# Attention and feed-forward on one core: work moved off GpSimd, layer norm moved a phase ahead, normalising moved behind both exps, closing tiles reordered

## The chip, the core and the metric

The kernel runs on one core of a Trainium2 chip. The core has TensorE (PE, matmuls), VectorE (DVE), ScalarE (ACT), GpSimd (POOL) and SyncE (SP), which here only issues transfers, and 16 DMA engines. Each engine works through its own list of instructions in order, and engines wait for each other by semaphores. The metric is the time of one execution on the device in microseconds.

## The reference

The input is normalised, goes through an attention in which each position sees itself and seven earlier positions two apart, and through a feed-forward net; the two results are multiplied and added to the input.

```python
def reference(A_x, A_wqkv, A_wo, B_x, B_w1, B_b1, B_w2, B_b2):   # x [1, 2048, 448], all bf16
    def _A_ref(x, wqkv, wo):
        H = 16; Dh = D // H;  W, dil = 8, 2
        q, k, v = ...                                   # (x @ wqkv), heads of 28
        idx = pos[:, None] - (jnp.arange(W) * dil)[None, :];  mask = idx >= 0
        ...
        logits = jnp.einsum("bhsd,bhswd->bhsw", q, kg) * Dh ** -0.5
        attn = _softmax(jnp.where(mask[None, None, :, :], logits, -1e9), axis=-1)
        o = jnp.einsum("bhsw,bhswd->bhsd", attn, vg)
        return o.transpose(0, 2, 1, 3).reshape(B, S, D) @ wo
    def _B_ref(x, w1, b1, w2, b2):                      # F = 1792
        h = _gelu(jnp.einsum("bsd,df->bsf", x, w1) + b1)
        return jnp.einsum("bsf,fd->bsd", h, w2) + b2
    x = A_x
    xn = _layernorm(x, axis=-1)
    s = _A_ref(xn, A_wqkv, A_wo)
    g = _silu(_B_ref(xn, B_w1, B_b1, B_w2, B_b2))
    return x + s * g
```

## The kernel before

**Tiles.** The 2048 rows are put in order of even and odd rows, so that the seven earlier positions become neighbours. They are worked on as 16 tiles of 128 rows (`t`), as four chunks of 512 columns (`c`, NC = 4) for the matmuls that need the transposed input, and as 17 attention units of QB = 121 queries (`b`), each with its 128 keys. `xnT` holds the normalised input transposed, `qT` and `kT` queries and keys transposed, `vw` the values of a unit with a column of ones ahead of each head, by which the attention matmul gives the softmax denominator too.

**Steps.** `ln_stats`, `ln_rstd`, `ln_apply`: mean and variance on VectorE (L157, L158), the reciprocal root by Ln and Exp on ScalarE (L161, L162), the normalising on VectorE (L165, with a small copy L168). `ln_tr`, `ln_put`: four transposes on TensorE (L173) and a copy out of PSUM. `qk_weights`: eight copies that lay the q and k weights `wraw` out anew as `wqk` (L183, VectorE). `q_job`, `k_job`, `v_job`: four matmuls each (L189, L204) and a copy out (q on VectorE, k and v on ScalarE). `qk_unit`: 16 small matmuls S (L296), and twice an exp on ScalarE (L301) with a mask multiply on VectorE (L303). `av_unit`: 16 small matmuls psO (L312), a `stream_shuffle` that spreads the denominator (`den`, L316), and `norm`, which is handed back to be placed later: Ln and Exp of den on ScalarE (L319, L320) and the multiply into `oT` on VectorE (L321). `feed_forward_1`: per chunk 14 output tiles of 512 columns (L225, L234), gelu on ScalarE (L240). `ffn2_job`: 14 matmuls (L258) and the bias add `y` on VectorE (L260). `silu_job`: Tanh on ScalarE (L264) and a multiply-add `g` on VectorE (L265). `wo_job`: four matmuls (L272), `sg` (L278) and the sum with x, `o_t` (L281), both on VectorE, then the store (L282).

**Order.** Everything from L368 on stands in a block in which TensorE, VectorE, ScalarE and GpSimd run in the order in which the code is written. SyncE's queue and what stands ahead of the block are put in place by a scheduler. The program is: a start (tiles 0 to 3, v 0 to 3, weight copies, q and k of chunk 0, the first tiles of FFN1); three phases c = 0, 1, 2, each of `feed_forward_1(c)`, with the transposes of the next chunk in it, and of five attention units, four of which have an `ffn2_job` and a q, k or v job beside them, while the fifth has two v jobs and the first tiles of the next FFN1; then `feed_forward_1(3)` and a closing with units 15 and 16 and the last four tiles. Exp and Ln are in one table set of ScalarE, Gelu and Tanh in another, so that each phase loads tables twice (L335, L363). In `qk_unit` the `norm` of the unit before is placed between the two exps (L305).

**PSUM.** The pool psA has two buffers (S, odd tiles of FFN1). The pool psB has four banks that go round among transposes, v, q, k, FFN1, ffn2, wo and psO (tag "B"): whoever takes a bank waits for the reader of its last content.

**GpSimd** sets constants: `late_constants` (L125) has 34 memsets for `vw`, the masks `mk`, the memset of `wo`, and then issues wo's 16 loads on its own queue. In the closing it adds `o_t` of tiles 13 and 14 (L461, L463).

## Time and profile before

| | us |
|---|---|
| median of 3 runs | 190.26 (189.57 to 190.98) |
| the profiled execution | 189.0 |
| its span | 187.2 |
| PE busy (matmuls) | 167.3 (89%) |
| PEld busy (weight loads) | 75.8 (40%) |
| DVE busy | 121.2 (65%) |
| ACT busy | 124.5 (66%) |
| POOL busy | 17.3 (9%) |

Busy time is summed over the whole span, and matmuls are pipelined, so a busy TensorE is not TensorE at its peak. A row of the timeline gives the start of a group of like instructions, how long the group took, engine, line, operation and tiles; in brackets stand the idle time of the engine just before it and what released it. Starts count from the start of the span. A row of the chain gives start, length and the work that the end of the program waited for. Lines (L...) are those of the kernel above.

### The profile page before, as it was taken

The numbers are of one execution on the slowest core, as the hardware profiler recorded it, in microseconds if no ns is written. First come the engines' busy times: TensorE is split into PE (matmuls) and PEld (weight loads), VectorE is DVE, ScalarE is ACT, GpSimd is POOL, SyncE is SP. The second block draws the span as 40 slices with busy tenths as digits, with TensorE's granted clock in tenths as the row PEclk, the third lists the DMA queues.
The fourth block names the chain that finished last, engine by engine and source line by source line (L and its number), as shares of the span: only waits on it lengthen the run. The fifth ranks groups of instructions, "written<-read, shape, count | busy, mean of one in ns | idle before, by whom it ended". The sixth has DMA issues, their size and how long they took to land.

```text
span 187.2 us, 3332 instructions
## 1 busy us (share of the span) xinstructions
PE 167.3 (89%) x1324; PEld 75.8 (40%) x1324; DVE 121.2 (65%) x255; ACT 124.5 (66%) x195; POOL 17.3 (9%) x75
## 2 busy tenths in 40 slices
PE   7759989999998699999998689999998999999940
PEld 2314334444443244344543334444443344454510
DVE  3875754838677577838775656828677426887693
ACT  3833297196778798377778895096877799753610
POOL 2088760000000000000000000000000000000022
PEclk9999999999999999999999999999999999999995
DMA  5999940000000000000000001000000000310012
GB/s 155 214 314 327 368 121 4 2 2 4 0 4 0 0 0 4 0 0 0 4 0 4 2 0 49 0 28 0 4 0 0 4 2 0 123 53 25 0 49 74
DMA packets 10831, 9.04 MB, mean 48 GB/s; under 512 B 2656, under 2 KB 10816, under 8 KB 10816
## 3 DMA queue, kind: packets, MB, share of 16 engines
q1 hardware_dynamic: 10016, 8.21, 14.5%
q0 software_dynamic: 512, 0.40, 0.8%
q8 instruction: 10, 0.16, 0.4%
q10 hardware_dynamic: 288, 0.23, 0.4%
q14 instruction: 5, 0.04, 0.1%
HBM read 7.00 MB, written 1.84 MB: 47 GB/s over the span
## 4 chain that ended last, share of the span: by engine, by line
PE 37%; ACT 35%; DVE 18%; DMA 3%; issue 2%; SPq 1%; POOL 0%; DVEq 0%; ACTq 0%; POOLq 0%
ACT E L301 13%; PE ps_h L225 12%; PE ps_qk L189 10%; ACT hT L240 7%; ACT den L320 5%; ACT den L319 4%; DVE E L303 4%; DMA wraw<-in_A_wqkv_dram 3%; PE ps_h L234 3%; PE psO L312 3%; PE ps_y L258 3%; PE S L296 3%; DVE g L265 2%; DVE sg L278 2%; ACT L363 2%
## 5 line engine op out<-in xcount | busy, mean ns | idle before, releaser
L240 ACT ACTIVATE hT<-ps_h,b1f 128x512 bf16<-128x512 f32 x56 | 34.4, 700 | 16.7 <-PE ps_h L234 15.9
L258 PE MATMUL ps_y<-w,hT 128*128 128x448 bf16 x224 | 45.1, 353 | 0.0
L225 PE MATMUL ps_h<-xnT,w 128*128 128x512 bf16 x168 | 41.5, 380 | 2.1 <-DVE oT L321 1.9
L301 ACT ACTIVATE E<-S 128x976 bf16<-128x976 f32 x34 | 32.8, 978 | 9.9 <-PE S L296 9.8
L189 PE MATMUL ps_qk<-xnT,wqk 128*128 128x512 bf16 x128 | 30.0, 380 | 2.0 <-DVE wqk L183 2.0
L303 DVE TENSOR_TENSOR E<-E,mk_gen 128x976 bf16<-128x976 bf16 x30 | 20.1, 669 | 14.3 <-ACT E L301 14.0
L258 PEld LDWEIGHTS <-hT 128*128 128x128 bf16 x224 | 20.7, 98 | 19.2
L225 PEld LDWEIGHTS <-w 128*128 128x128 bf16 x168 | 15.0, 98 | 22.9 <-issue 5.0
L189 PEld LDWEIGHTS <-wqk 128*128 128x128 bf16 x128 | 12.2, 98 | 17.0 <-DVE wqk L183 2.7
L321 DVE TENSOR_TENSOR oT<-psO,den 128x484 bf16<-128x484 f32 (+1 forms) x17 | 11.2, 661 | 11.7 <-ACT den L320 11.7
L265 DVE SCALAR_TENSOR_TENSOR g<-th,y 128x448 bf16<-128x448 bf16 x16 | 10.2, 672 | 11.0 <-ACT th L264 11.0
L192 DVE CAST qT<-ps_qk 128x512 bf16<-128x512 f32 x16 | 11.0, 686 | 9.4 <-PE ps_qk L189 9.3
L281 POOL TENSOR_TENSOR o_t<-x,sg 128x448 bf16<-128x448 bf16 x2 | 2.1, 1028 | 154.5 <-DVE sg L278 154.5
L204 PE MATMUL ps_v<-wv,xnT 128*128 128x448 bf16 x68 | 15.2, 353 | 0.1
L319 ACT ACTIVATE den<-den 128x484 f32<-128x484 f32 (+1 forms) x17 | 10.2, 601 | 6.8 <-DVE den L316 6.7
L272 PE MATMUL ps_s<-wo,oT 128*128 128x448 bf16 x64 | 13.8, 353 | 0.9 <-ACT hT L240 0.8
L316 DVE STREAM_SHUFFLE den<-psO 128x484 f32<-128x484 f32 (+1 forms) x17 | 11.8, 693 | 0.0
L192 ACT CAST kT<-ps_qk 128x512 bf16<-128x512 f32 x10 | 5.8, 582 | 8.5 <-PE ps_qk L189 4.9
L209 ACT CAST vw<-ps_v 128x448 bf16<-128x448 f32 x17 | 8.7, 534 | 3.9 <-PE ps_v L204 3.8
L264 ACT ACTIVATE th<-y 128x448 bf16<-128x448 f32 x16 | 8.6, 598 | 3.8 <-DVE y L260 3.8
L157 DVE BATCH_NORM_STATS2 st<-x 128x6 f32<-128x448 bf16 x16 | 9.7, 608 | 2.1 <-DMA x<-in_A_x_dram 2.1
L320 ACT ACTIVATE den<-den 128x484 f32<-128x484 f32 (+1 forms) x17 | 10.3, 605 | 0.5
(58 smaller groups left out, 155.1 us busy)
## 6 DMA issues: line engine op xcount, KB each, us to landing
out_dram<-o_t SPq DMA_DIRECT2D x16, 112.0 KB, 1.7
w<-in_B_w_dram SPq DMA_DIRECT2D x1, 1568.0 KB, 10.4
w<-in_B_w_dram SPq DMA_DIRECT2D x2, 672.0 KB, 7.7
x<-in_A_x_dram SPq DMA_DIRECT2D x3, 448.0 KB, 7.9
wraw<-in_A_wqkv_dram SPq DMA_DIRECT2D x1, 672.0 KB, 6.1
w<-in_B_w_dram SPq DMA_DIRECT2D x4, 112.0 KB, 6.1
wo<-in_A_wo_dram POOLq DMA_DIRECT2D x16, 24.5 KB, 4.8
wv<-in_A_wqkv_dram SPq DMA_DIRECT2D x1, 336.0 KB, 4.7
```

The lines of the kernel that those rows point to most:

```text
L189: nc.tensor.matmul(ps[:, :], wqk[:, kt, 16 * which + 4 * g:16 * which + 4 * g + 4, :], xnT[:, kt, LEAD + c * CH:LEAD + (c + 1) * CH], star ...
L192: copy((qT, kT)[which][:, g, LEAD + c * CH:LEAD + (c + 1) * CH], ps[:, :])
L204: nc.tensor.matmul(ps[:, :], xnT[:, kt, o:o + P], wv[:, kt, :], start=(kt == 0), stop=(kt == KT - 1))
L225: nc.tensor.matmul(ps[i][:, :], w1[:, kt, m * P:(m + 1) * P], xnT[:, kt, LEAD + c * CH:LEAD + (c + 1) * CH], start=(first and kt == 0), st ...
L240: nc.scalar.activation(hT[:, m, :], ps[i][:, :], ACT.Gelu_apprx_tanh, bias=b1f[:, m:m + 1])
L258: nc.tensor.matmul(ps[:, :], hT[:, m, tt * P:(tt + 1) * P], w2[:, m, :], start=(m == 0), stop=(m == MT - 1))
L265: nc.vector.scalar_tensor_tensor(out=g_sb[t % NG][:], in0=th[:], scalar=1.0, in1=y_sb[:, t % 4, 0:D], op0=ALU.add, op1=ALU.mult)
L272: nc.tensor.matmul(ps[:, :], oT[:, g, t * P:(t + 1) * P], wo[:, g, :], start=(g == 0), stop=(g == 3))
L301: nc.scalar.activation(ev, Sp[p2][:, :, :, 0:QW], ACT.Exp, scale=SCALE)
L303: nc.vector.tensor_tensor(out=ev, in0=ev, in1=mkb, op=ALU.mult)
L319: nc.scalar.activation(den[:, :, 0:n], den[:, :, 0:n], ACT.Ln)
L320: nc.scalar.activation(den[:, :, 0:n], den[:, :, 0:n], ACT.Exp, scale=-1.0)
```

## The change

1. GpSimd: `vw` becomes one tile, and its 34 memsets become two that stand early. The memsets of `wv`, `wraw`, `wo`, `qT`, `kT` and `mk_gen` go to VectorE; wo's 16 loads go to SyncE's queue; the cast of `b1f` goes to the end of `late_constants`; both `o_t` adds of the closing go to VectorE.
2. Layer norm: the statistics of tiles 4 to 7 stand among the q and k jobs of the start, and their `ln_apply` behind the first FFN1 tiles, ahead of `feed_forward_1(0)`. In the phases `ln_apply` of the next chunk but one stands in the first four units.
3. Units: `norm` of the unit before stands behind both exps. In the fifth unit a v job is placed between the exps, and the second v job ahead of `norm`.
4. Closing: tile 12's silu is made with Exp, Ln and Exp between the units' `norm`; matmuls and put of wo and ffn2 are apart and in another order.

```diff
-    vw = [big.tile([P, H, 32], BF16, name=f"vw_{b}") for b in range(NB)]
+    vw = big.tile([P, NB, H, 32], BF16, name="vw")
...
-    nc.gpsimd.memset(wv[64:128, 3, :].bitcast(U32), 0)
-    nc.gpsimd.memset(wraw[:, :, 2 * D:2 * D + 8].bitcast(U32), 0)
-    nc.gpsimd.memset(wraw[64:128, 3, 0:2 * D].bitcast(U32), 0)
+
+    nc.gpsimd.memset(vw[:, :, :, 0:1], 1.0)
+    nc.gpsimd.memset(vw[:, :, :, DH + 1:32], 0.0)
+    nc.vector.memset(wv[64:128, 3, :].bitcast(U32), 0)
+    nc.vector.memset(wraw[:, :, 2 * D:2 * D + 8].bitcast(U32), 0)
+    nc.vector.memset(wraw[64:128, 3, 0:2 * D].bitcast(U32), 0)
+    nc.vector.memset(wo[:, :, :].bitcast(U32), 0)
+    for tl in (qT, kT):
+        nc.vector.memset(tl[:, :, 0:LEAD].bitcast(U32), 0)
+        nc.vector.memset(tl[:, :, LEAD + S:LQ].bitcast(U32), 0)
+    for g in range(4):
+        for h in range(4):
+            r = (4 * g + h) * DH
+            nc.sync.dma_start(wo[32 * h + 1:32 * h + 1 + DH, g, :], A_wo[r:r + DH, :])
 
     def late_constants():
-        nc.gpsimd.tensor_copy(b1f[:], b1t[:])
-        for tl in (qT, kT):
-            nc.gpsimd.memset(tl[:, :, 0:LEAD].bitcast(U32), 0)
-            nc.gpsimd.memset(tl[:, :, LEAD + S:LQ].bitcast(U32), 0)
-        for b in range(NB):
-
-            nc.gpsimd.memset(vw[b][:, :, 0:1], 1.0)
-            nc.gpsimd.memset(vw[b][:, :, DH + 1:32], 0.0)
-
-        nc.gpsimd.memset(mk_gen[:], 1.0)
+
+        nc.vector.memset(mk_gen[:], 1.0)
...
-        nc.gpsimd.memset(wo[:, :, :].bitcast(U32), 0)
-        for g in range(4):
-            for h in range(4):
-                r = (4 * g + h) * DH
-                nc.gpsimd.dma_start(wo[32 * h + 1:32 * h + 1 + DH, g, :], A_wo[r:r + DH, :])
+        nc.gpsimd.tensor_copy(b1f[:], b1t[:])
...
+    def silu_exp_job(t):
+
+        e = work.tile([P, D], F32, name="se", tag="se", bufs=1)
+        nc.scalar.activation(e[:], y_sb[:, t % 4, 0:D], ACT.Exp, scale=-1.0)
+        nc.scalar.activation(e[:], e[:], ACT.Ln, bias=1.0)
+        nc.scalar.activation(e[:], e[:], ACT.Exp, scale=-1.0)
+
+        def put():
+            nc.vector.scalar_tensor_tensor(out=g_sb[t % NG][:], in0=e[:], scalar=2.0, in1=y_sb[:, t % 4, 0:D],
+                                           op0=ALU.mult, op1=ALU.mult)
+        return put
...
             if p2 == 0:
-                norm()
+                between()
...
                     ln_put(nx + j, ln_tr(nx + j), nc.vector.tensor_copy)
-                    if j + 2 < 4:
-                        ln_apply(nx + j + 2)
...
         for g in range(4):
             q_job(0, g)
+            if g == 3:
+                ln_stats(7)
+                ln_rstd(4, 4)
+            else:
+                ln_stats(4 + g)
             k_job(0, g)
+        ps = ffn1_even(0, 0)
         for t in range(4, 8):
-            ln_stats(t)
-        ln_rstd(4, 4)
-        ps = ffn1_even(0, 0)
-        ln_apply(4)
-        ln_apply(5)
+            ln_apply(t)
...
                 b = next(units)
-                E = qk_unit(b, norm)
+                E = qk_unit(b)
+                norm()
                 ffn2_job(4 * c + i)
                 beside[i]()
+                if n + 1 < NC:
+                    ln_apply(4 * n + 4 + i)
                 norm = av_unit(b, E)
             b = next(units)
-            E = qk_unit(b, norm)
-            v_job(4 * n + 2 + (c == 2))
-            v_job(4 * n + 3 + (c == 2))
+            va, vb = 4 * n + 2 + (c == 2), 4 * n + 3 + (c == 2)
+            E = qk_unit(b, lambda: v_job(va))
+            v_job(vb)
+            norm()
             ps = ffn1_even(n, 0)
             norm = av_unit(b, E)
             norm()
-            if n + 1 < NC:
-                ln_apply(4 * n + 4)
-                ln_apply(4 * n + 5)
         feed_forward_1(3, ps, [3, 4, 5, 6, 7])
         wo_job(8)
         E = qk_unit(15)
         ffn2_job(12)
-        wo_job(9)
+        s9 = wo_mm(9)
         norm = av_unit(15, E)
-        E = qk_unit(16, norm)
+        wo_put(9, s9)
+        E = qk_unit(16)
+        norm()
+        g12 = silu_exp_job(12)
         ffn2_job(13)
-        wo_job(10)
+        g12()
+        s10 = wo_mm(10)
         norm = av_unit(16, E)
         norm()
+        wo_put(10, s10)
         nc.scalar.preload_act_table_set(SET_GELU)
-        silu_job(12)
+        s11 = wo_mm(11)
+        y14 = ffn2_job(14, False)
+        wo_put(11, s11)
+        s12 = wo_mm(12)
+        ffn2_put(14, y14)
+        wo_put(12, s12)
         silu_job(13)
-        ffn2_job(14)
-        wo_job(11)
         silu_job(14)
-        wo_job(12)
-        ffn2_job(15)
         s13 = wo_mm(13)
-        wo_put(13, s13, nc.gpsimd)
+        wo_put(13, s13)
+        y15 = ffn2_job(15, False)
+        s14 = wo_mm(14)
+        s15 = wo_mm(15)
+        ffn2_put(15, y15)
+        wo_put(14, s14)
         silu_job(15)
-        wo_job(14, nc.gpsimd)
-        wo_job(15)
+        wo_put(15, s15)
```

VectorE in the start, where tiles 1 to 3 are normalised (xnb_75 to xnb_77; x_70 is the first chunk of x) and the weights are laid out anew. Before:

```order
L165 TENSOR_SCALAR xnb_75<-x_70,mv,rstd 128x448
L168 COPY xnb_75<-xnb_75 128x64
L157 BN_STATS st<-x_70 128x6
L158 BN_AGGR mv<-st 128x2
L165 TENSOR_SCALAR xnb_76<-x_70,mv,rstd 128x448
L168 COPY xnb_76<-xnb_76 128x64
L165 TENSOR_SCALAR xnb_77<-x_70,mv,rstd 128x448
L168 COPY xnb_77<-xnb_77 128x64
L183 COPY wqk<-wraw 128x512 x8
L192 CAST qT<-ps_qk 128x512 x4
```

After:

```order
L164 TENSOR_SCALAR xnb_75<-x_70,mv,rstd 128x448
L167 COPY xnb_75<-xnb_75 128x64
L156 BN_STATS st<-x_70 128x6
L157 BN_AGGR mv<-st 128x2
L125 MEMSET wraw 128x4x4
L164 TENSOR_SCALAR xnb_76<-x_70,mv,rstd 128x448
L167 COPY xnb_76<-xnb_76 128x64
L164 TENSOR_SCALAR xnb_77<-x_70,mv,rstd 128x448
L167 COPY xnb_77<-xnb_77 128x64
L182 COPY wqk<-wraw 128x512 x8
```

The memset of wraw's last columns, which stood on GpSimd, now stands on VectorE ahead of the normalising of tile 2.

ScalarE in the first phase, from the v copy of the fourth unit to the load of the gelu tables. Before:

```order
L209 CAST vw_86<-ps_v 128x16x28
L301 ACTIVATE E<-S 128x8x122
L319 ACTIVATE den<-den 128x484
L320 ACTIVATE den<-den 128x484
L301 ACTIVATE E<-S 128x8x122
L209 CAST vw_87<-ps_v 128x16x28
L209 CAST vw_88<-ps_v 128x16x28
L319 ACTIVATE den<-den 128x484
L320 ACTIVATE den<-den 128x484
L335 ACT_TABLE_LOAD
```

After:

```order
L208 CAST vw<-ps_v 128x16x28
L317 ACTIVATE E<-S 128x8x122
L208 CAST vw<-ps_v 128x16x28
L317 ACTIVATE E<-S 128x8x122
L208 CAST vw<-ps_v 128x16x28
L335 ACTIVATE den<-den 128x484
L336 ACTIVATE den<-den 128x484
L335 ACTIVATE den<-den 128x484
L336 ACTIVATE den<-den 128x484
L351 ACT_TABLE_LOAD
```

The fifth unit's two exps now have a v copy between them, and the Ln and Exp of the fourth unit stand behind both v copies, right ahead of those of the fifth.

VectorE at the end of the program, the last twelve rows. Before (g_100 to g_103 and g_111 are silu results, x_72 and x_73 chunks of x):

```order
L260 TENSOR_TENSOR y<-ps_y,b2bc 128x448
L278 SCALAR_TENSOR_TENSOR sg<-ps_s,g_111 128x448
L281 TENSOR_TENSOR o_t<-x_72,sg 128x448
L265 SCALAR_TENSOR_TENSOR g_102<-th,y 128x448
L278 SCALAR_TENSOR_TENSOR sg<-ps_s,g_100 128x448
L281 TENSOR_TENSOR o_t<-x_73,sg 128x448
L260 TENSOR_TENSOR y<-ps_y,b2bc 128x448
L278 SCALAR_TENSOR_TENSOR sg<-ps_s,g_101 128x448
L265 SCALAR_TENSOR_TENSOR g_103<-th,y 128x448
L278 SCALAR_TENSOR_TENSOR sg<-ps_s,g_102 128x448
L278 SCALAR_TENSOR_TENSOR sg<-ps_s,g_103 128x448
L281 TENSOR_TENSOR o_t<-x_73,sg 128x448
```

After:

```order
L294 SCALAR_TENSOR_TENSOR sg<-ps_s,g_84 128x448
L297 TENSOR_TENSOR o_t<-x_73,sg 128x448
L269 SCALAR_TENSOR_TENSOR g_85<-th,y 128x448
L269 SCALAR_TENSOR_TENSOR g_86<-th,y 128x448
L294 SCALAR_TENSOR_TENSOR sg<-ps_s,g_85 128x448
L297 TENSOR_TENSOR o_t<-x_73,sg 128x448
L264 TENSOR_TENSOR y<-ps_y,b2bc 128x448
L294 SCALAR_TENSOR_TENSOR sg<-ps_s,g_86 128x448
L297 TENSOR_TENSOR o_t<-x_73,sg 128x448
L269 SCALAR_TENSOR_TENSOR g_87<-th,y 128x448
L294 SCALAR_TENSOR_TENSOR sg<-ps_s,g_87 128x448
L297 TENSOR_TENSOR o_t<-x_73,sg 128x448
```

All the sums `o_t` of tiles 12 to 15 are VectorE's now, and the matmuls' results of one tile are taken up (sg, then o_t) ahead of the y of a later one; of the silu multiplies three stand in the last twelve, since that of tile 12 is no longer near them and those of 13 and 14 have come later.

## Rows read from the trace of the kernel before

**Rows 1.** The page, part 4: shares of the chain that ended last, by engine

```profile
PE 37%; ACT 35%; DVE 18%; DMA 3%; issue 2%; SPq 1%; POOL 0%; DVEq 0%; ACTq 0%; POOLq 0%
```

**Rows 2.** Timeline of the start: start, length, engine, line, work, count, [idle before, releaser]

```profile
0.93 0.27 DVE L96 MEMSET wz<- 128x256 uint32 x1 [0.93 <-PEq L478]
...
3.35 0.63 DVE L157 BATCH_NORM_STATS2 st<-x 128x6 f32<-128x448 bf16 x1 [2.14 <-DMA x<-in_A_x_dram]
...
7.33 0.37 DVE L165 TENSOR_SCALAR xnb<-x,mv,rstd 128x448 bf16<-128x448 bf16 x1
...
8.84 0.70 DVE L183 COPY wqk<-wraw 128x512 bf16<-128x512 bf16 x3 [0.19 <-DMA wraw<-in_A_wqkv_dram]
...
9.94 0.11 POOL L122 MEMSET wraw<- 128x16 uint32 x1 [8.10 <-DMA wraw<-in_A_wqkv_dram]
...
10.61 3.92 DVE L183 COPY wqk<-wraw 128x512 bf16<-128x512 bf16 x5 [1.07 <-POOL wraw L123]
...
10.84 1.03 PE L189 MATMUL ps_qk<-xnT,wqk 128*128 128x512 bf16 x4
...
13.44 0.27 POOL L135 MEMSET mk_gen<- 128x122 bf16 x1
...
13.90 6.27 PE L189 MATMUL ps_qk<-xnT,wqk 128*128 128x512 bf16 x28 [2.04 <-DVE wqk L183]
...
24.04 0.96 PE L173 MATMUL pT<-ident,xnb 128*128 128x128 bf16 x8 [0.62 <-DVE xnb L165]
```

**Rows 3.** The page, part 5: all shuffles of the denominator (busy, mean ns)

```profile
L316 DVE STREAM_SHUFFLE den<-psO 128x484 f32<-128x484 f32 (+1 forms) x17 | 11.8, 693 | 0.0
```

**Rows 4.** The chain that ended last, in a middle unit: start, length, work

```profile
49.99 0.61 ACT den L320
50.59 0.88 ACT E L301
```

**Rows 5.** Timeline of TensorE, the same unit

```profile
48.05 0.39 PE L296 MATMUL S<-qT,kT 28*128 28x122 bf16 x16
...
51.88 0.73 PE L312 MATMUL psO<-E,vw 128*32 128x122 bf16 x16
52.55 0.40 PE L296 MATMUL S<-qT,kT 28*128 28x122 bf16 x16
```

**Rows 6.** Timeline of TensorE and ScalarE at the ends of phases

```profile
57.05 0.39 PE L296 MATMUL S<-qT,kT 28*128 28x122 bf16 x16
...
60.36 0.96 ACT L209 CAST vw<-ps_v 128x448 bf16<-128x448 f32 x2
...
63.86 1.28 ACT L335 ACT_TABLE_LOAD   x1
...
64.90 0.97 PE L173 MATMUL pT<-ident,xnb 128*128 128x128 bf16 x8 [1.37 <-DVE xnb L165]
65.71 0.59 PE L225 MATMUL ps_h<-xnT,w 128*128 128x512 bf16 x2
...
111.17 1.69 PE L272 MATMUL ps_s<-wo,oT 128*128 128x448 bf16 x8 [0.76 <-ACT hT L240]
```

**Rows 7.** Timeline of VectorE in the closing

```profile
173.56 0.62 DVE L321 TENSOR_TENSOR oT<-psO,den 128x448 bf16<-128x448 f32 x1 [1.26 <-ACT den L320]
...
178.02 0.62 DVE L265 SCALAR_TENSOR_TENSOR g<-th,y 128x448 bf16<-128x448 bf16 x1
178.56 0.62 DVE L278 SCALAR_TENSOR_TENSOR sg<-ps_s,g 128x448 bf16<-128x448 f32 x1
179.21 0.39 DVE L281 TENSOR_TENSOR o_t<-x,sg 128x448 bf16<-128x448 bf16 x1
179.52 0.61 DVE L260 TENSOR_TENSOR y<-ps_y,b2bc 128x448 f32<-128x448 f32 x1
...
183.36 0.79 DVE L281 TENSOR_TENSOR o_t<-x,sg 128x448 bf16<-128x448 bf16 x1
```

**Rows 8.** Windows: stretch, length, busy PE, PEld, DVE, ACT, POOL, PEclk, DMA share, GB/s

```profile
182.80:187.20 4.40, 0.00 (x0) 0.00 (x0) 1.31 (x2) 0.00 (x0) 1.03 (x1) 0.50 0.20 68
```

More of the change, by code (lines that the diff above doesn't have):

```diff
@@ L208, in v_put @@
     def v_put(b, ps):
-        nc.scalar.copy(vw[b][:, :, 1:DH + 1], ps[:, :].rearrange("p (h c) -> p h c", h=H))
+        nc.scalar.copy(vw[:, b, :, 1:DH + 1], ps[:, :].rearrange("p (h c) -> p h c", h=H))
     def v_job(b):
@@ L252, in ffn1_odd, with ffn2_job @@
         return ps
-    def ffn2_job(t):
+    def ffn2_job(t, put=True):
         tt = t % 4
@@ L259, in ffn2_job, with ffn2_put @@
                              start=(m == 0), stop=(m == MT - 1))
-        nc.vector.tensor_tensor(out=y_sb[:, tt, 0:D], in0=ps[:, :], in1=b2bc[:], op=ALU.add)
+        if put:
+            ffn2_put(t, ps)
+        return ps
+    def ffn2_put(t, ps):
+        nc.vector.tensor_tensor(out=y_sb[:, t % 4, 0:D], in0=ps[:, :], in1=b2bc[:], op=ALU.add)
     def silu_job(t):
@@ L274, in wo_mm, with wo_put @@
         return ps
-    def wo_put(t, ps, eng=None):
+    def wo_put(t, ps):
         sg = work.tile([P, D], BF16, name="sg", tag="sg", bufs=3)
@@ L280, in wo_put, with wo_job, qk_unit @@
         o_t = work.tile([P, D], BF16, name="o_t", tag="o_t", bufs=3)
-        (eng or nc.vector).tensor_tensor(out=o_t[:], in0=xt(t), in1=sg[:], op=ALU.add)
+        nc.vector.tensor_tensor(out=o_t[:], in0=xt(t), in1=sg[:], op=ALU.add)
         nc.sync.dma_start(dram_rows(out_par, t, 1)[:, 0, :], o_t[:])
-    def wo_job(t, eng=None):
-        wo_put(t, wo_mm(t), eng)
-    def qk_unit(b, norm=lambda: None):
+    def wo_job(t):
+        wo_put(t, wo_mm(t))
+    def qk_unit(b, between=lambda: None):
         E = work.tile([P, 4, 4, P], BF16, name="E", tag="E", bufs=2)
@@ L311, in av_unit @@
             for h in range(4):
-                nc.tensor.matmul(psO[32 * h:32 * h + 32, g, 0:QW], vw[b][:, 4 * g + h, :],
+                nc.tensor.matmul(psO[32 * h:32 * h + 32, g, 0:QW], vw[:, b, 4 * g + h, :],
                                  E[:, h, g, 0:QW], start=True, stop=True)
```

## The prediction

> **What bounds the kernel now.** I read the page's chain first, then the stretches that it names. Of the chain that ended last TensorE holds 37%, ScalarE 35% and VectorE 18% [rows 1]: no engine is the bound alone, the chain changes hands, so I sum by stage what is on it. The sum is made against the profiled execution, 189.0 us (span 187.2, the rest around it); the median, 190.26, is 0.7% above it, so the result is scaled by 1.0067 at the end.
>
> In the start the reader is to see TensorE empty for 2.04 us at 13.90, for the copies of the q and k weights on VectorE. Three copies took 0.70 us together, five took 3.92: one of them stood still for some 3.0 us, and it came free when the dense run of GpSimd's memsets ended at 13.44 + 0.27 [rows 2]. In a middle attention unit TensorE's list begins anew every 52.55 − 48.05 = 4.50 us, and of this the 16 psO matmuls took 0.73, against 0.40 and 0.39 for the 16 S matmuls [rows 5]: TensorE waits 0.33 inside, for the mask of the second exp. That exp stands behind the Ln and Exp of the unit before [rows 4]. At the end of a phase 65.71 − 57.05 = 8.66 us pass from the fifth unit's S to the next full tile of FFN1, among them a wait of 1.37 for VectorE's layer norm [rows 6]. At the end VectorE is the last engine, up to 183.36 + 0.79 = 184.15 [rows 7].
>
> **Start: 34 small memsets gone, but one memset now on VectorE.** The stuck copy has nothing dense to stand behind any more: 3.0 us come free. But the memset of wraw's last columns, which waits for both loads of wraw and began at 9.94 on GpSimd, where 8.10 us of waiting hurt nobody [rows 2], stands in the new order on VectorE between the statistics of tile 3 and the normalising of tile 2. Behind it are queued the normalising of tiles 2 and 3 and the eight weight copies; behind those TensorE's transposes, v 1 to 3 and all q and k. That normalising began at 7.33 before; now it begins at 9.94 + 0.11 = 10.05. From it to the first q matmul there were 10.84 − 7.33 = 3.51 us of this chain's own work, so q may begin at 13.56. The copies begin 8.84 − 7.33 = 1.51 after it, at 11.56, and are done 8 x 0.23 later at 13.4: just in time. The 32 matmuls of q and k, at 6.27 / 28 = 0.22 each, end at 20.6; before, the last 28 began at 13.90 and FFN1 followed at about 20.1. So 0.5 is lost. TensorE's wait of 0.62 at 24.04 for tiles 4 and 5 goes, since their normalising now stands ahead of FFN1. Net gain 0.1.
>
> The other memsets moved to VectorE are some 1,700 words; by the row with 256 words in 0.27 us an estimate of 1.8 us. They are hidden by the 2.14 us that VectorE waits for x at 3.35 [rows 2]; without this cover they cost at most 1.8. I take zero, and 1.8 goes to the range. The two large memsets of vw and the late cast of b1f are on GpSimd, idle for 8 us there; wo's loads go to SP behind the x loads, and wo is first needed about 90 us later. These I cost at nothing, at most 0.3.
>
> The rule that bears on this is in the Trainium skill, SBUF — State Buffer, "SBUF: two separate sides": of VectorE and GpSimd whichever begins first holds the shared port pair for the whole instruction, and the other blocks until it is done. Read strictly, one memset can hold a copy for one memset's time only, the stuck 3 us would have another cause, and would stay. The trace differs: the copy sat through some forty memsets, which overlap, and not through one. By the rule the sum would be 2.8 worse; it is rival F.
>
> **Units: normalising behind both exps.** The second exp no longer waits for Ln and Exp of the unit before, about 1.2 us on ScalarE [rows 4]. So the mask and psO no longer hold TensorE, and the 0.33 goes: the unit is then bound by TensorE's own list, 4.17. Next late is the normalising itself: oT of the unit before comes some 0.9 later, and its PSUM bank is wanted by the ffn2 of the next unit. I find a margin of about 0.3 us, the closest point of the change. VectorE's list in a unit (two masks, oT, den, y, and now one ln_apply of 0.4 to 0.6) is about 3.9, so it stays under 4.17. Gain 0.33 in units 2 to 4 of the first two phases and two of the third: 8 x 0.33 = 2.6. Ends: nothing, and 8 x 0.5 if the exps pull the masks still further ahead.
>
> **Phase ends.** ln_apply leaves the stretch behind the fifth unit; what is late next is oT of the fifth unit itself, whose bank the second transpose needs. From S on: first exp at 0.4, exp 0.88, v copy 0.48, exp 0.88, v copy 0.48 (two took 0.96 [rows 6]), which is 3.1; Ln and Exp of the fourth unit at 0.6 each [rows 4], 4.3; its oT 0.62 [rows 7], 4.95; den of the fifth unit 0.69 [rows 3], 5.65; its Ln and Exp, 6.85; its oT, 7.5; four transposes, half of 0.97, and the next tile stands at about 7.9, against 8.66. Gain 0.8 in the first phase. In the second 0.2 is lost again, since the wo matmuls that follow waited 0.76 for gelu anyway, and that wait is not shortened as much [rows 6]: 0.6. In the third the next work is gelu: the table load began 63.86 − 57.05 = 6.8 after S in the first phase [rows 6], and would begin at 6.85 now: nothing. Together 1.4; bounds 0 to 2.7.
>
> **Closing.** Unit 16's normalising comes at the same moment, its oT at 173.56. After it VectorE has, in the new order, oT 0.62, six sg at 0.65, six o_t (five at 0.31, the last 0.39), two y at 0.53 and three g at 0.54 (start to start, [rows 7]): 9.1 us, so 182.7 instead of 184.15, if nothing of it waits. Gain 1.4. The three passes of the new silu of tile 12 are 3 x 0.6 of ScalarE, between the two units' normalising; they are covered while unit 16's psO and den are still under way. Without that cover they cost up to 1.8.
>
> **Sum.** 0.1 + 2.6 + 1.4 + 1.4 = 5.5; 189.0 − 5.5 = 183.5; scaled, 184.7 us.
>
> **Rivals.**
> A. The start is freed in full: the memset does not hold VectorE, or the loads of wraw end earlier now that nothing else is queued. Then q begins at 10.84 and another 2.7 is gained: 182.0. Against it: the load released GpSimd at 9.94, and nothing ahead of it in its queue is changed.
> B. TensorE's clock falls in the new empty stretch of the start, some 2.7 us before tile 2's transposes. At half rate 16 of the 32 matmuls would take 0.22 more each, 3.5: 188.2. For it: after the last matmuls the granted clock was 0.50, that is 1.2 GHz instead of 2.4 [rows 8]. Against it: after the empty 2.04 at 13.90 the 28 matmuls ran at 0.22 each [rows 2]. That idleness lowers the clock is also in the Trainium skill, TensorE: Matmul & The Clock Gate, "What's actually happening"; the trace agrees for the end of the span, and not for this shorter stretch.
> C. The units do not shorten, as the bank of the unit before last comes free too late and ffn2 waits where psO waited: 2.6 less, 187.3. For it: the margin of 0.3 is of the size of two instruction gaps. Against it: ScalarE and VectorE keep 0.3 to 0.6 of slack in a unit.
> D. The closing gains nothing, because the three passes delay unit 16's Ln, or TensorE's wo 12 to 15 arrive late: 186.1.
> E. The other side: the clock falls to half at each of the long waits that the change makes, the one of the start and one of about 1.7 for oT at the end of each of the first two phases. At 3.5 each, 10.5 against a gain of 5.5: 195.2. The second fall takes the gain away, the third decides. Against it: waits of 2.04 and 1.37 cost no clock before [rows 2, 6].
> F. The stuck copy stays: 2.8 more, 187.5.
>
> **How the numbers follow.** Forecast 0.55, A 0.05, B 0.10, C 0.10, D 0.09, E 0.05, F 0.06. The likeliest's own range is 183.2 to 186.3 (0.5 to 1.5 either way from the memsets, the phase ends and the closing). The range for 8 in 10 takes in A to D and F: 181.9 to 188.2; what it leaves out is E and the edges of A and B, about 0.15. One per cent, about what a measurement of this kernel can tell from no change, is 188.4 on the near side and 192.2 on the far side. Faster holds the forecast, A, C, D, F and half of B: 0.90; same the other half of B: 0.05; slower E: 0.05.
>
> **What would show it.** In the profile after: in the start VectorE's memset of wraw waiting for the DMA until about 9.9, eight copies in under 2.2 us, and the first q matmul near 13.5 with all q and k at 0.22; in a middle unit 16 psO matmuls in 0.4 and 4.2 us from S to S; at the first two phase ends about 7.9 from S to the next full tile and a wait for oT ahead of the second transposes; at the end VectorE without a gap from oT of unit 16 on. The prediction is wrong if the units still take 4.5, if a wait for oT stands ahead of ffn2, if q begins before 12 or after 15, or if any stretch with matmuls shows a granted clock near 0.5.

## The result and the profile after

The changed kernel takes 184.31 us (median of 4 runs, 183.85 to 185.27); the kernel before took 190.53 beside it (189.57 to 190.98). The ratio is 0.9687, 95% interval 0.9631 to 0.9742. The prediction was 184.7. The profiled execution took 184.2 with a span of 182.6, against 189.0 and 187.2. Beside the experiments the kernel before took 188.5 to 189.8 where the mean granted clock of TensorE over the execution was 0.986 to 0.994, and 190.6 to 192.0 where it was 0.979 to 0.983; its profiled execution (189.0, clock 0.988) is like the former, which is probably why the profiled executions lie 4.8 apart and the medians 6.2.

The S matmuls of the 17 units are good marks: from one S to another a stage can be measured in any of the kernels. The table is made of their starts in the timeline of TensorE (us; each kernel's profiled execution).

| | before | after | gained | forecast |
|---|---|---|---|---|
| first q matmul | 10.84 | 15.21 | −4.37 | −2.72 |
| first matmul of FFN1 | 20.02 | 22.12 | −2.10 | −0.5 |
| S of unit 0 | 38.75 | 39.71 | −0.96 | +0.1 |
| units 0 to 4 | 18.30 | 17.29 | 1.01 | |
| units 5 to 9 | 18.30 | 17.30 | 1.00 | |
| units 10 to 14 | 18.29 | 17.64 | 0.65 | the three: 2.6 |
| unit 4 to 5 (phase end and FFN1) | 22.57 | 21.78 | 0.79 | 0.8 |
| unit 9 to 10 | 25.77 | 25.15 | 0.62 | 0.6 |
| units 14 to 16 | 23.91 | 24.00 | −0.09 | 0 |
| unit 16 to the end of the span | 21.31 | 19.73 | 1.58 | 1.4 |
| together | 187.2 | 182.6 | 4.6 | 5.5 |

All terms but one came out to within 0.2; the start came out a microsecond worse. What stood in [rows 2] is now, in the timeline of the start (rows of VectorE and TensorE; "..." marks rows left out):

```profile
6.84 0.92 PE L203 MATMUL ps_v<-wv,xnT 128*128 128x448 bf16 x4
...
9.47 0.07 DVE L125 MEMSET wraw<- 128x16 uint32 x1 [2.01 <-DMA wraw<-in_A_wqkv_dram]
9.47 0.40 DVE L164 TENSOR_SCALAR xnb<-x,mv,rstd 128x448 bf16<-128x448 bf16 x1
...
9.93 0.61 PE L172 MATMUL pT<-ident,xnb 128*128 128x128 bf16 x4 [2.17 <-DVE xnb L164]
...
10.33 1.70 PE L203 MATMUL ps_v<-wv,xnT 128*128 128x448 bf16 x4
...
10.51 1.70 DVE L182 COPY wqk<-wraw 128x512 bf16<-128x512 bf16 x8
...
12.25 3.13 PE L203 MATMUL ps_v<-wv,xnT 128*128 128x448 bf16 x8
...
15.21 7.07 PE L188 MATMUL ps_qk<-xnT,wqk 128*128 128x512 bf16 x31
...
22.12 1.46 PE L224 MATMUL ps_h<-xnT,w 128*128 128x512 bf16 x6
```

The memset waits for the load on VectorE, the normalising of tile 2 behind it, TensorE 2.17 behind that: as forecast. The eight copies run without a stop. But v 0 took 0.92 for four matmuls ahead of the empty stretch, and v 1 took 1.70 behind it. The windows (columns as in [rows 8]) tell why: the granted clock fell in the stretch, between 8.0 and 8.5, and was 0.50, that is 1.2 GHz, until q began.

```profile
5.00:10.00 5.00, 1.72 (x13) 0.88 (x14) 2.82 (x12) 2.88 (x9) 0.00 (x0) 0.84 0.89 198
10.00:15.00 5.00, 5.00 (x20) 2.57 (x21) 2.31 (x12) 2.14 (x4) 1.47 (x6) 0.50 1.03 327
15.00:20.00 5.00, 4.95 (x24) 2.21 (x24) 3.08 (x7) 1.71 (x3) 0.00 (x0) 0.98 1.09 326
```

In a middle unit psO no longer waits (0.40 where [rows 5] had 0.73), and S follows S after 4.17:

```profile
48.67 0.39 PE L312 MATMUL S<-qT,kT 28*128 28x122 bf16 x16
...
52.51 0.40 PE L328 MATMUL psO<-E,vw 128*32 128x122 bf16 x16
52.84 0.40 PE L312 MATMUL S<-qT,kT 28*128 28x122 bf16 x16
```

At the phase end 64.87 − 57.00 = 7.87 pass where [rows 6] had 8.66, with the forecast wait for oT in the middle:

```profile
57.00 0.39 PE L312 MATMUL S<-qT,kT 28*128 28x122 bf16 x16
...
62.52 0.39 PE L172 MATMUL pT<-ident,xnb 128*128 128x128 bf16 x4
64.63 0.40 PE L172 MATMUL pT<-ident,xnb 128*128 128x128 bf16 x4 [1.73 <-DVE oT L337]
64.87 1.46 PE L224 MATMUL ps_h<-xnT,w 128*128 128x512 bf16 x6
```

In the closing VectorE runs from oT of unit 16 to the last sum in 179.33 + 0.39 − 170.48 = 9.24, nearly without a gap (forecast 9.14; [rows 7] had 10.59):

```profile
170.48 0.62 DVE L337 TENSOR_TENSOR oT<-psO,den 128x448 bf16<-128x448 f32 x1 [1.26 <-ACT den L336]
...
179.33 0.39 DVE L297 TENSOR_TENSOR o_t<-x,sg 128x448 bf16<-128x448 bf16 x1
```

### The profile page after: what moved, and what is told of

It is laid out like the page before. It is cut to its first block, busy times and chain, and to the rows that moved or that the text cites. A ratio compares the mean times of both kernels' runs of the same rounds, so it can differ in the third digit from the quotient of the medians.

```text
span 182.6 us, 3260 instructions
## 1 busy us (share of the span) xinstructions
PE 165.5 (91%) x1308; PEld 76.6 (42%) x1324; DVE 118.0 (65%) x266; ACT 125.3 (69%) x197; POOL 4.6 (2%) x16
## 3 DMA queue, kind: packets, MB, share of 16 engines
q1 hardware_dynamic: 10688, 8.61, 15.8%
## 4 chain that ended last, share of the span: by engine, by line
PE 60%; ACT 24%; DVE 8%; DMA 3%; issue 2%; SPq 1%; DVEq 0%
PE ps_y L257 18%; PE ps_qk L188 12%; PE ps_h L224 11%; ACT E L317 6%; PE ps_v L203 5%; ACT hT L239 5%; PE ps_s L288 4%; DMA wraw<-in_A_wqkv_dram 3%; PE S L312 3%; ACT den L336 3%; PE ps_h L233 3%; ACT den L335 2%; PE psO L328 2%; DVE sg L294 2%; DVE g L269 2%
## 5 line engine op out<-in xcount | busy, mean ns | idle before, releaser
L224 PE MATMUL ps_h<-xnT,w 128*128 128x512 bf16 x160 | 40.4, 380 | 0.6 <-DVE sg L294 0.2
L317 ACT ACTIVATE E<-S 128x976 bf16<-128x976 f32 x34 | 32.0, 986 | 7.3 <-PE S L312 6.3
L188 PE MATMUL ps_qk<-xnT,wqk 128*128 128x512 bf16 x120 | 29.2, 379 | 0.4
L224 PEld LDWEIGHTS <-w 128*128 128x128 bf16 x168 | 15.2, 98 | 20.1 <-issue 4.8
L269 DVE SCALAR_TENSOR_TENSOR g<-th,y 128x448 bf16<-128x448 bf16 x15 | 8.7, 621 | 13.7 <-ACT th L268 13.7
L203 PE MATMUL ps_v<-wv,xnT 128*128 128x448 bf16 x68 | 17.2, 392 | 0.0
L172 PE MATMUL pT<-ident,xnb 128*128 128x128 bf16 x64 | 6.1, 232 | 6.9 <-DVE oT L337 3.4
L233 PE MATMUL ps_h<-xnT,w 64*128 64x512 bf16 x56 | 9.9, 383 | 0.5 <-ACT hT L239 0.2
L294 DVE SCALAR_TENSOR_TENSOR sg<-ps_s,g 128x448 bf16<-128x448 f32 x16 | 9.9, 616 | 0.2
```

The costliest lines, as they stand in the source:

```text
L188: nc.tensor.matmul(ps[:, :], wqk[:, kt, 16 * which + 4 * g:16 * which + 4 * g + 4, :], xnT[:, kt, LEAD + c * CH:LEAD + (c + 1) * CH], star ...
L203: nc.tensor.matmul(ps[:, :], xnT[:, kt, o:o + P], wv[:, kt, :], start=(kt == 0), stop=(kt == KT - 1))
L224: nc.tensor.matmul(ps[i][:, :], w1[:, kt, m * P:(m + 1) * P], xnT[:, kt, LEAD + c * CH:LEAD + (c + 1) * CH], start=(first and kt == 0), st ...
L233: nc.tensor.matmul(ps[i][:, :], w1[r, 3, m * P:(m + 1) * P], xnT[r, 3, LEAD + c * CH:LEAD + (c + 1) * CH], start=first, stop=not first)
L294: nc.vector.scalar_tensor_tensor(out=sg[:], in0=ps[:, :], scalar=0.5, in1=g_sb[t % NG][:], op0=ALU.mult, op1=ALU.mult)
L317: nc.scalar.activation(ev, Sp[p2][:, :, :, 0:QW], ACT.Exp, scale=SCALE)
```

## Experiments

The kernel before ran beside each experiment (medians 189.2 to 190.7), so the kernels are compared by their ratio to it, and stages by one profiled execution of each.

### The start: the clock, the memset, the small memsets

**a_busy.** Nine matmuls of zeros fill the empty stretch.

```diff
         v0 = v_mm(0)
+        busy(9)
```

> The changed kernel with nine more matmuls of zeros (512 columns) behind v 0, in the stretch in which TensorE stands empty from 7.76 to 9.93 in the start; their result is read by nobody. Theory: the clock fell in that stretch, and that cost 12 v matmuls 0.19 each and the transposes some 0.2. With the stretch filled they run at full rate, the first q matmul stands near 12.9 instead of 15.21, and the time is 184.3 - 2.2 = 182.1. Rival: the v matmuls were slow for another cause (the transfers at full load there, or the copies out of PSUM): they stay at 0.38, and the time stays 184.3.

Measured: 182.78, ratio 0.9642 (0.9588 to 0.9696). The intervals of this ratio and of the changed kernel's overlap; the timeline of the start shows the difference (VectorE's memset first, then TensorE):

```profile
10.07 0.07 DVE L125 MEMSET wraw<- 128x16 uint32 x1 [2.57 <-DMA wraw<-in_A_wqkv_dram]
...
7.63 2.11 PE L347 MATMUL ps_w<-wz 128*128 128x512 bf16 x9
...
10.80 0.92 PE L203 MATMUL ps_v<-wv,xnT 128*128 128x448 bf16 x4
...
11.78 1.98 PE L203 MATMUL ps_v<-wv,xnT 128*128 128x448 bf16 x8
13.60 7.07 PE L188 MATMUL ps_qk<-xnT,wqk 128*128 128x512 bf16 x32
20.51 1.46 PE L224 MATMUL ps_h<-xnT,w 128*128 128x512 bf16 x6
```

With the stretch filled, v 1 to 3 run at full rate, and from the release of the memset (10.07 here, 9.47 in the changed kernel) to the first q matmul there are 3.53 us and not 5.74. The forecast chain had 3.51. The clock cost 2.2 us; the load, which landed 0.6 later in this execution, took a part of it back.

**a_tail.** The one memset goes back to GpSimd, all else as changed.

```diff
-    nc.vector.memset(wraw[:, :, 2 * D:2 * D + 8].bitcast(U32), 0)
+    nc.gpsimd.memset(wraw[:, :, 2 * D:2 * D + 8].bitcast(U32), 0)
```

> The changed kernel with one line different: the memset of wraw's last columns is back on GpSimd. Theory: nothing holds VectorE, tile 2 is normalised at 7.4, there is no empty stretch and no fall of the clock; the copies begin when wraw has landed (about 9.5) and the first q matmul stands at 10.5 to 11, FFN1 at 17.6 to 18.1 instead of 22.12: 4.0 to 4.5 less, 179.8 to 180.3. Rival: the weights and the x of FFN1 and of tiles 4 to 7 are not there before about 20, so that FFN1 waits for transfers: 2.1 less, 182.2. Second rival: the wait only moves to the copies, TensorE is empty from about 9 to 11 and the clock falls all the same: 183 to 184.

Measured: 181.20, ratio 0.9547 (0.9481 to 0.9612). This is 1.4 points better than the changed kernel, but some 1 us short of the theory. The empty stretch is gone; q stands at 12.41 and not at 10.5 to 11:

```profile
6.91 1.70 PE L203 MATMUL ps_v<-wv,xnT 128*128 128x448 bf16 x4
...
10.61 1.97 PE L203 MATMUL ps_v<-wv,xnT 128*128 128x448 bf16 x8
12.41 7.23 PE L188 MATMUL ps_qk<-xnT,wqk 128*128 128x512 bf16 x32
...
16.28 0.63 DVE L156 BATCH_NORM_STATS2 st<-x 128x6 f32<-128x448 bf16 x1 [2.11 <-DMA x<-in_A_x_dram]
```

Here v 0 and v 1 ran at half rate from the outset. That belongs to the execution and not to the edit: a_best below has the same start and its first q matmul at 10.85. The statistics of tile 4 wait 2.11 for x on VectorE, with a q copy queued behind them; from the first q matmul to FFN1 7.06 us pass, against 6.91 in the changed kernel. So the rival of the loads holds for 0.15 us here (7.68 pass in a_best, where q begins earlier).

**b_gps and b_gps_tail.** The kernel before with part 1 of the change alone, but for the two sums of the closing, which stay on GpSimd; and the same with that one memset left on GpSimd (the line of a_tail).

> The kernel before with the GpSimd part of the change alone (34 memsets to two, memsets to VectorE, wo's loads to SyncE). Theory: the start loses as in the changed kernel: TensorE empty for 2.2 us before tile 2's transposes, clock at half until about 15, FFN1 at about 22 and not 20.0: 2 us more, 192.3 to 192.8 against 190.5. Rival: the stuck copy was worth more than the stall: 188 to 190.5.

> The same part alone, but with the memset of wraw's last columns left on GpSimd. Theory: the copies run without a stop, the first q matmul stands at 10.8 and the 28 behind it follow at once: 3.0 less at the start of q and k, of which TensorE's waits for x of tiles 4 to 7 may give back a part: 187.5 to 188.5 against 190.5. Rival: FFN1 then waits for its weights: 190.5.

Measured: b_gps 190.64, ratio 1.0066 (1.0022 to 1.0109), slower by less than a per cent; the 0.9 to 1.2 per cent that were expected lie at the edge of the interval. In its profiled execution, 1.2 above that median, S of unit 0 stands 2.9 later than before and the first q matmul at 15.80; v 0 took 1.70 there, half rate ahead of the empty stretch already. b_gps_tail took 186.65, ratio 0.9821 (0.9742 to 0.9900), an interval that holds what was expected; S of unit 0 stands 2.2 earlier. Its timeline:

```profile
6.83 0.92 PE L203 MATMUL ps_v<-wv,xnT 128*128 128x448 bf16 x4
...
10.88 7.07 PE L188 MATMUL ps_qk<-xnT,wqk 128*128 128x512 bf16 x31
17.78 1.46 PE L224 MATMUL ps_h<-xnT,w 128*128 128x512 bf16 x6
```

One line turns the GpSimd part from a small loss into a gain; the two medians lie 2.1% apart.

**b_two.** The 34 memsets become two in the place where they stood (`vw` is one tile).

```diff
-            nc.gpsimd.memset(vw[b][:, :, 0:1], 1.0)
-            nc.gpsimd.memset(vw[b][:, :, DH + 1:32], 0.0)
+        nc.gpsimd.memset(vw[:, :, :, 0:1], 1.0)
+        nc.gpsimd.memset(vw[:, :, :, DH + 1:32], 0.0)
```

> The kernel before with the 34 memsets of vw made two in the same place on GpSimd (272 and 816 elements, 1.3 us each in the changed kernel), all else as before. Theory: what held the weight copy was a dense run of GpSimd instructions that overlap: two memsets that follow each other hold it for up to 2.5 us, so little is gained, 0.5 to 1: 189.5 to 190.0. Rival (one instruction is waited for, then the copy goes): at most one memset of 1.3 holds it: 1.7 less, 188.8. Second rival: memsets do not hold it at all: the copies take as long as before, 190.5.

Measured: 189.14, ratio 0.9975 (0.9930 to 1.0020): nothing that shows. The copies on VectorE (the last line has the shortest, median and longest of the eight in ns) and the memsets beside them:

```profile
10.59 3.91 DVE L181 COPY wqk<-wraw 128x512 bf16<-128x512 bf16 x5 [0.81 <-POOL wraw L123]
...
11.31 1.28 POOL L130 MEMSET vw<- 128x272 bf16 x1
12.19 1.58 POOL L131 MEMSET vw<- 128x816 bf16 x1
13.65 0.22 POOL L133 MEMSET mk_gen<- 128x122 bf16 x1
...
L181 DVE COPY wqk<-wraw x8: 274/290/3016, 9.1 to 14.1; 128x512 bf16<-128x512 bf16 x8
```

The longest copy takes 3.02 as before (3.03), beside a series of GpSimd instructions of which each begins ahead of the end of the last, whether they are many or few. It ends at 14.02, 0.15 after the memset of `mk_gen`, the last of the series; in the kernel before it ends at 13.85, 0.14 after the same memset. In both the next GpSimd instruction begins only behind the end of this one. So it is not the number of memsets, nor is one instruction waited for, as the first rival had it. The second rival has the time right, but not the cause: in b_gps_tail, with the memsets gone from beside them, the same eight copies take 2.12 together. Which instructions of the series can hold a copy is not shown. Part 1 gains by having moved the memsets to a time when VectorE waits for x.

### Units and phase ends

**b_norm.** The normalising behind both exps alone, in the kernel before.

```diff
-                E = qk_unit(b, norm)
+                E = qk_unit(b)
+                norm()
                 ffn2_job(4 * c + i)
...
-            E = qk_unit(b, norm)
+            E = qk_unit(b)
             v_job(4 * n + 2 + (c == 2))
             v_job(4 * n + 3 + (c == 2))
+            norm()
```

> The kernel before with one part of the change alone: the normalising behind both exps in the four units and behind the two v copies in the fifth. Theory: 8 units at 4.17 and not 4.50, 2.7 less; the phase ends gain nothing or lose up to 0.5 each, since ln_apply still stands there and oT of the fourth unit comes later: 188.0 to 189.0 against 190.5. Rival: the bank of the unit before last comes free too late without layer norm's move and the units stay at 4.5: 190.5.

Measured: ratio 0.9929 (0.9879 to 0.9979), under one per cent. The units take 17.29, 17.30 and 17.64 from first to fifth, to 0.01 those of the changed kernel: this part alone makes the units' 2.66. But the stages of the phase ends grow from 22.57 to 24.24 and from 25.77 to 26.56, far more than the 0.5 that was expected. VectorE and TensorE at the first:

```profile
62.70 0.66 DVE L321 TENSOR_TENSOR oT<-psO,den 128x484 bf16<-128x484 f32 x1 [1.31 <-ACT den L320]
63.28 0.39 DVE L165 TENSOR_SCALAR xnb<-x,mv,rstd 128x448 bf16<-128x448 bf16 x1
...
63.73 0.96 PE L173 MATMUL pT<-ident,xnb 128*128 128x128 bf16 x8 [1.99 <-DVE xnb L165]
64.53 2.21 PE L225 MATMUL ps_h<-xnT,w 128*128 128x512 bf16 x6
66.67 1.03 PE L234 MATMUL ps_h<-xnT,w 64*128 64x512 bf16 x4
```

The later oT pushes ln_apply, which stands behind it, and the transposes wait for that; but from S of the fifth unit they come only 0.09 later than before (7.94 against 64.90 − 57.05 = 7.85). The other 1.58 lie behind them: after the empty 1.99 the granted clock was 0.50 from about 65.1 to 68.5, and the first six matmuls of FFN1 took 2.21 where the changed kernel has 1.46. At the second phase end it is the same: 0.08 ahead of the transposes, 0.71 behind, clock 0.50 from about 106.1 to 109.5 after an empty 1.99. So it is TensorE's clock that gives back most of what the units gained.

**a_between.** The changed kernel with the normalising between the exps again.

```diff
-                E = qk_unit(b)
-                norm()
+                E = qk_unit(b, norm)
```

> The changed kernel with the normalising of the unit before placed between the two exps again, in the four units of a phase alone (the fifth unit and the closing as changed). Theory: a unit takes 4.50 again and not 4.17, 16 psO matmuls 0.73 and not 0.40: 8 x 0.33 = 2.7 more, 187.0. Rival: the units became shorter because layer norm left the stretches around them: 184.3.

Measured: 188.19, ratio 0.9922 (0.9883 to 0.9962). The units take 18.86, 18.86 and 18.31, together 3.8 more than in the changed kernel, and not 2.7. The units of the third phase, which have no ln_apply, are as before; those of the other two are longer than before by 0.56 in all, because ln_apply now stands on VectorE ahead of the shuffle of den, for which the Ln between the exps waits on ScalarE. In the unit that begins at 44.55 this wait is 0.51, and psO waits for the mask:

```profile
49.34 0.39 PE L328 MATMUL psO<-E,vw 128*32 128x122 bf16 x14 [0.62 <-DVE E L319]
```

So alone, normalising behind both exps brought 2.7 in the units and lost 2.5 at the phase ends (b_norm); beside the layer norm's move it is worth 3.8 in the units and loses nothing there. The layer norm's move without it (a_between, which keeps the new order of the fifth unit) costs 1.1 in the units against the kernel before, and gains 1.4 at the phase ends.

**a_slow.** Each unit's normalising made some 0.6 us later.

```diff
             nc.scalar.activation(den[:, :, 0:n], den[:, :, 0:n], ACT.Exp, scale=-1.0)
+            nc.scalar.copy(den[:, :, 0:n], den[:, :, 0:n])
```

> The changed kernel with a copy of den onto itself on ScalarE (some 0.6 us) between each unit's Exp and its oT. It measures how much later oT can come before a unit grows. Theory: the margin is about 0.3, so a unit grows by 0.3 from 4.17 and the four units of a phase take 18.2 and not 17.3; the two phase ends grow by up to 1.2 each and the closing by 0.6. Rival: the margin is over 0.6, and the units stay at 17.3.

Measured (one profiled execution): units 17.51, 17.50 and 17.75, some 0.05 more each and not 0.3. So oT may come about 0.55 later before a unit grows; the margin of 0.3 was an underestimate. The two phase ends grow by 2.9 and 1.3, and both waits for oT there from 1.73 to 2.84 and 2.83:

```profile
66.53 0.60 PE L172 MATMUL pT<-ident,xnb 128*128 128x128 bf16 x4 [2.84 <-DVE oT L338]
66.93 2.76 PE L224 MATMUL ps_h<-xnT,w 128*128 128x512 bf16 x6
...
108.70 0.40 PE L172 MATMUL pT<-ident,xnb 128*128 128x128 bf16 x4 [2.83 <-DVE oT L338]
```

The two waits are alike, the outcome is not: behind the first the granted clock was 0.50 from about 66.6 to 70.0, behind the second it stayed at 1.00 and the same six matmuls of FFN1 took 1.46. The fall cost 1.6. The two stages behind unit 14 grow by 1.25 and 1.24, without a fall; for the closing 0.6 was expected.

### Closing, and two ways to a faster kernel

**a_close.** The changed kernel with the closing's former order (its calls as in lines 442 to 464 of the kernel before), but norm behind both exps and all sums on VectorE.

> The changed kernel with the order of the closing of before (tile 12's silu by Tanh, wo and ffn2 jobs in one piece each), but with normalising behind both exps and all sums on VectorE as in the changed one. Theory: the closing's gain, 1.58 by the two traces (from the S of unit 16 to the end 21.31 before, 19.73 after), goes, less what GpSimd's two slow sums had cost: 185.0 to 185.9. Rival: the gain came from taking the two sums of 1.03 each off GpSimd alone: 184.3.

Measured: 185.64, ratio 0.9788 (0.9731 to 0.9844). By stages of the profiled execution, the quickest of its four, 20.28 pass from unit 16 to the end, against 19.73 with the new order and 21.31 before. So of the 1.58 the order and the new silu make 0.55, and what a_close shares with the changed kernel 1.03: 0.22 up to oT of unit 16, the other 0.81 behind it, where the two sums no longer stand on GpSimd. In a_close VectorE still waits 1.26 for the table load and Tanh behind oT:

```profile
170.57 0.62 DVE L337 TENSOR_TENSOR oT<-psO,den 128x448 bf16<-128x448 f32 x1 [1.26 <-ACT den L336]
172.46 1.16 DVE L269 SCALAR_TENSOR_TENSOR g<-th,y 128x448 bf16<-128x448 bf16 x2 [1.26 <-ACT th L268]
```

In the kernel before, beside the two sums on GpSimd, one g on VectorE took 1.43 and not 0.62, and the last o_t 0.79 and not 0.39 [rows 7]:

```profile
180.75 1.03 POOL L281 TENSOR_TENSOR o_t<-x,sg 128x448 bf16<-128x448 bf16 x1 [153.38 <-DVE sg L278]
180.83 1.43 DVE L265 SCALAR_TENSOR_TENSOR g<-th,y 128x448 bf16<-128x448 bf16 x1 [0.17 <-ACT th L264]
...
182.87 1.03 POOL L281 TENSOR_TENSOR o_t<-x,sg 128x448 bf16<-128x448 bf16 x1 [1.09 <-DVE sg L278]
```

**a_best and a_best2.** a_tail with the second tile's transposes behind the next FFN1 tiles, to fill the wait of 1.73; and the same with two more matmuls of zeros in the start.

```diff
                 ps = ffn1_even(c, k)
                 gelu(k, ps)
+                if k == 2 and c + 1 < NC:
+                    ln_put(nx + 1, ln_tr(nx + 1), nc.vector.tensor_copy)
...
-                for j in (k, k + 1):
+                for j in ((0,), (2, 3))[k // 2]:
```

> The kernel of a_tail, and in each phase the transposes of the next chunk's second tile stand behind the next two tiles of FFN1 instead of ahead of them. Theory: the wait of 1.73 for oT of the fifth unit, which the change made at two phase ends, is filled with FFN1; from the S of the fifth unit to the next phase's first S 20.05 instead of 21.78 in the first phase, and 23.4 instead of 25.15 in the second; 3.4 less than a_tail: 177.8. Rival: the wait moves to gelu on ScalarE, which cannot begin before the table load behind the fifth unit's Exp, and FFN1 stops at its next tile for a free PSUM buffer: 0.5 to 1 less each, 179.5 to 180.

> The kernel of a_best with two more matmuls of zeros in the start: nine instead of eight ahead of the first transposes, and one behind them, where TensorE stood empty for 0.4 and 0.6. Theory: in a_tail the first eight v matmuls took 0.37 each and the rest 0.23, so the clock came up only near 10.6, and what keeps TensorE from standing empty before brings it up sooner: the first q matmul at 10.9 and not at 12.4, 1.5 less: 176.3. Rival: when the clock comes up is a matter of the execution and not of these gaps: as a_best.

Measured: 182.40, ratio 0.9582 (0.9485 to 0.9680), and 182.38, ratio 0.9586 (0.9506 to 0.9667). Both miss: they are no faster than a_tail. The stages of the phase ends grow to 23.12 and 25.49: the wait for oT is gone, 0.58 for gelu has come, and 1.73 for a copy of xnT that now stands on VectorE behind the g of two silu jobs:

```profile
62.56 0.37 PE L233 MATMUL ps_h<-xnT,w 64*128 64x512 bf16 x1 [0.58 <-ACT hT L239]
...
64.74 1.16 DVE L269 SCALAR_TENSOR_TENSOR g<-th,y 128x448 bf16<-128x448 bf16 x2 [3.20 <-ACT th L268]
65.82 1.32 DVE L176 COPY xnT<-pT 128x512 bf16<-128x512 bf16 x3
...
66.29 0.38 PE L172 MATMUL pT<-ident,xnb 128*128 128x128 bf16 x4 [1.73 <-DVE xnT L176]
```

In both the first q matmul stands at 10.85 or 10.81, where a_tail with the same start has 12.41, so what the two extra matmuls do can't be told from what differs between executions.

**a_all.** a_best2 with the silu jobs behind that copy, and the statistics of tiles 4 to 7 behind the third and fourth k job.

```diff
                 gelu(k, ps)
+                if k == 2:
+                    if c + 1 < NC:
+                        ln_put(nx + 1, ln_tr(nx + 1), nc.vector.tensor_copy)
+                    if c:
+                        silu_job(4 * (c - 1))
+                        silu_job(4 * (c - 1) + 1)
...
             k_job(0, g)
+            if g == 2:
+                ln_stats(4)
+            if g == 3:
+                for t in (5, 6, 7):
+                    ln_stats(t)
+                ln_rstd(4, 4)
```

> The kernel of a_best2 with two mends: the silu jobs that stood ahead of the second tile's copy out of PSUM on VectorE stand behind it, and the statistics of tiles 4 to 7, which waited for x with a q copy queued behind them, stand behind the third and fourth k job. Theory: of the waits that a_best showed, 0.62 for the q copy and 1.73 for the copy of xnT go and 0.58 for gelu stays: FFN1 at 17.8 to 18.0, 20.6 from the S of the fifth unit to the next phase's S (21.78 in the changed kernel, 23.12 in a_best) and 24.0 (25.15, 25.49); 181.2 - 1.5 - 2.3 = 177.4. Rival: Tanh, now behind two more gelus, makes ScalarE late at the next FFN1 tiles, and the phase ends gain nothing: 179.7.

Measured: 180.29, ratio 0.9533 (0.9437 to 0.9629), 2.9 above the theory. FFN1 begins at 17.82 as expected, the first phase end gains 0.55 against the changed kernel (21.23), and the second loses 0.67 (25.82): the wo matmuls there now wait 2.17 for gelu, where in the changed kernel they waited 0.95 for a copy of xnT.

```profile
104.88 1.68 PE L288 MATMUL ps_s<-wo,oT 128*128 128x448 bf16 x8 [2.17 <-ACT hT L239]
```

a_all and a_tail beat both kernels; by their intervals they can't be told apart, and a_tail is one line.

## Why the prediction was right, and where it was not

**Right: units, phase ends, closing.** The units' 0.33 is the whole effect of normalising behind both exps (b_norm makes it alone, a_between takes it back and 1.1 more), TensorE's own list of 4.17 is what is left, and rival C was further off than said (a_slow). The list of the phase end, 7.9 from S, was met to 0.03, with oT of the fifth unit the last; the third phase end is 0, as said. VectorE's closing list was met to 0.1. The memsets moved to VectorE, taken as zero, took 1.8 there under the wait for x: the first statistics began at 3.40, before at 3.35. Rivals A and D did not come: the memset held VectorE until 9.47, and the closing gained.

**Wrong: the step "so q may begin at 13.56".** The chain of waits was right: 3.51 us from the normalising of tile 2 to q, and a_busy has 3.53. The load even released the memset 0.47 earlier than was taken (9.47 against 9.94). But the term took v 1 to 3 and the transposes at the full rate, and in the emptied stretch the clock fell. This is rival B, which had a chance of 0.10 and a price of 3.5 on the q and k matmuls. It came true at 2.2, on the 12 v matmuls and the transposes ahead of q; q and k themselves ran at 0.23 each. What spoke against rival B, that the wait of 2.04 in [rows 2] cost no clock, was a true row and a weak argument: a_slow has two waits of 2.84 and 2.83, one with a fall behind it and one without. That idleness lowers the clock is what the Trainium skill says in TensorE: Matmul & The Clock Gate, "What's actually happening"; the trace of the changed kernel agrees, in the stretch where the prediction thought it did not. The five profiled executions with this start (the changed kernel, a_between, a_close, a_slow, b_gps) have the first q matmul at 15.2 to 15.8. In four of them the clock is seen to fall; in b_gps v 0 was at half rate already. Two of the prediction's own signs of being wrong stand in these rows: q began after 15, and matmuls ran at a granted clock of 0.50.

**Rival E came in other kernels.** In the changed kernel the waits of 1.73 at the phase ends cost no clock (the matmuls behind them took 1.46 for six), as the prediction argued. But the clock did fall behind both phase ends of b_norm, after 1.99, and behind the first of a_slow.

**Mis-sized: what the start wins back.** With FFN1 2.10 late, unit 0 is only 0.96 late: 1.14 of waits in the first FFN1 went, not the 0.62 that was counted.

**Rival F fell, with that reading of the rule.** The stuck copy is gone. That the loser waits for one instruction of the other engine, as the rule was read from the Trainium skill, SBUF — State Buffer, "SBUF: two separate sides", is not what b_two shows: 3.02 us beside two long memsets, of 1.28 and 1.58, and what stood around them, as beside 34 short ones.

**Two errors cancel.** Between the profiled executions the gain is 4.8 us, where 5.5 were forecast. The scaling by 1.0067 then added 1.2, as if the profiled execution of the changed kernel were also below its median; it was at it (184.2 against 184.3). So the nearness of 184.7 to 184.31 is in part luck; the range does not rest on it.

## What to carry to other kernels

Look at what each moved instruction waits for, not only at what it costs: a memset of 0.07 us on the wrong queue cost more than 34 memsets saved, and one line made part 1 some 2% better. A stretch that empties TensorE can have a second price, the matmuls behind it at half rate. Here it was 0.7 to 2.2 us; it was paid after waits of 1.99, 2.17 and 2.84, and not after others of 1.73, 2.04 and 2.83. So it should stand in the sum, weighted, and not only among the rivals. A move can be worth next to nothing alone and 3.8 us beside another, as normalising behind both exps was, when it makes late what the other has taken out of the queue behind it.

## What the runs showed of the hardware

The clock at the beginning of an execution differs between executions whose start is the same: v 0 took 1.70 for its four matmuls in a_tail and 0.92 in a_best, and 1.70 in b_gps where the changed kernel has 0.92. In a_tail the profile prints a granted clock of 1.00 over that stretch all the same:

```profile
5.00:10.00 5.00, 4.10 (x20) 2.25 (x21) 3.49 (x13) 3.45 (x10) 0.00 (x0) 1.00 0.79 184
```

The first eight matmuls of zeros took 3.3 to 3.6 us wherever there were eight, nearly twice the 0.22 to 0.23 each of later ones of 512 columns, at a printed 1.00 too. So early in a span the speed is to be read from the matmuls' own durations. That the row stands at 1.00 until the first recorded change would explain it, but wasn't tried. What decides when the clock first comes up stays open; a_best and a_best2 did not separate it.
